# All w1 operands of the first MLP pass formed during the attention, drawn by an estimate of GpSimd's load; query tiles kept without memsets

## The chip, the core and the metric

The kernel runs on one core of a Trainium2 chip. A core has five engines that run side by side: TensorE (PE, with its weight loads as PEld), VectorE (DVE), ScalarE (ACT), GpSimd (POOL) and SyncE (SP). Each takes its instructions in program order and waits on semaphores for the others. In this kernel SP issues every DMA, so SP's order is the order in which transfers start, and a DMA that has to wait for its data holds all later ones.

The metric is the time of one execution in device microseconds (us). Before the change, three runs took 2300.64, 2301.75 and 2305.29 us; the median is 2301.75.

## What is computed

A transformer block with adaptive LayerNorm on x of 2048 x 576 in float32, with 32 query heads of width 18, one shared key and value head, and an MLP of width 4608:

```python
mod = (_silu(c) @ w_mod).reshape(c.shape[0], 6, 1, -1)
sa, ca, ga, sb, cb, gb = (mod[:, 0], mod[:, 1], mod[:, 2], mod[:, 3], mod[:, 4], mod[:, 5])
h = _layernorm(x, axis=-1) * (1 + ca) + sa
x = x + ga * _A_ref(h, A_wq, A_wk, A_wv, A_wo)
h = _layernorm(x, axis=-1) * (1 + cb) + sb
x = x + gb * _B_ref(h, B_w1, B_b1, B_w2, B_b2)
```

`_A_ref` is softmax attention. `_B_ref` applies its own LayerNorm, then `gelu(y @ w1 + b1) @ w2 + b2`.

## The kernel before, in words

**Precision.** Most products are made from parts: a float32 operand is split into a rounded high part and a rest ("hi" and "lo"), and three matmuls (hi x hi, hi x lo, lo x hi) replace one. Forming the parts is a cast and a subtraction. For weights POOL does it, in `two` (lines 692 to 696): `tensor_copy` at L694, `tensor_tensor` at L695.

**Stages.** Stage one (to about 130 us of the trace) does the first LayerNorm and the projections of q, k and v; q goes to the scratch `qscr` in DRAM. Stage two is the attention, to about 1422 us. Stage three is the MLP.

**The attention.** It runs over 32 query tiles n (four heads by 512 tokens each; eight tiles make a token block) and, in each, over 16 chunks kc of 128 keys. For each chunk there are four score matmuls (L824), four exponentials on ACT (L826) and the product with V into `psC` (L813). Beside them PE makes the scores of the next tile once more (L322, L834) so that DVE can take their row maxima (L846, L844), which the softmax needs before that tile starts.

A query tile sits in a buffer `qst`, of which there are three. `load_q(n + 2)` (L858) fills one in chunk 1 of tile n. Rows 0 to 53 of each half of 64 hold parts of q, rows 54 and 55 take the negated maxima, and the rest must be zero. Before the change `new_q` (L127) takes a fresh tile each time and POOL clears rows 32 to 63 of each half (L132). `smax_fin2` (L358), in chunk 13 of the tile before, negates the maxima (ACT L362, DVE L363) and SP writes them into rows 54 and 55 with four DMAs (L367). The scores of the tile wait for these.

**Finishing a tile.** `post_quad` (L613) is a generator that advances one step a chunk during the tile after. Chunk 0: ACT has copied `psC` to `O` (L619), and SP moves the row of sums to `R` (L637). Chunk 3: DVE's reciprocal (L641). Chunk 4: `R` goes to DRAM (`dsum`, L643). Chunk 5: it comes back broadcast as `T` (L647). Chunk 8: POOL multiplies (L651). Chunk 9: POOL makes two parts of the output (`os`, L661 and L662). Chunk 12: four DMAs put them in place for the output projection (`big<-os`, L668).

**Work beside the attention.** `between(n, kc)` (L848) is called once a chunk and sets the program order: the maxima of the next tile, a step of each finishing tile, `load_q`, then a step of `fill` in odd chunks (the late modulation weights, the output projection of a block that is complete, and for the first two blocks the second and third LayerNorm, `ln2_tile`, whose work is on POOL), then a step of `prep`. `prep` holds the generator `weight_parts` (L687): it loads raw weights, forms parts on POOL and sends them to the scratches `w1scr`, `w2scr` and `w2sum`. A store is issued in the step behind the one that formed its parts, and the parts have two buffers (`r2`), so POOL can form a third only when the first has landed in DRAM. Before the change `prep` gets one step in each chunk except 11 and 12, from tile 3 on, whatever else POOL has to do. What is left at chunk 8 of the last tile is emptied at once, and then the operands of the first MLP step are loaded (L867 to 871).

**The MLP.** It is a Strassen-like scheme: seven products of half size instead of eight, with seven operands of w1 (`OPS`, L676) that are blocks, sums and differences of blocks. It runs over two pairs of token blocks, and in each over 18 groups of 256 hidden units, 36 steps v in all; the first pass is v < 18. The operands of one step lie in `W1["r"]`. For groups 0, 1, 2 and 17 (`PRE`, L685) they were formed in the attention and are loaded from `w1scr`. For the other 14 the first pass loads the raw block (`raw_w1`), and POOL and ACT form the operands during the step before (`w1_part`, `w1_sum`, `tail_parts`), and SP stores them for the second pass, which loads all of them.

Of the kernel before, what the change touches and what calls it, by code (L numbers as in the profile page):

```python
# [18 lines left out]
KD = 5  # L19
# [9 lines left out]

@with_exitstack  # L30
def block_kernel(ctx: ExitStack, tc, x, wqkv, wo, w1, b1, w2, b2, c, wmod, ident_in, out):
    nc = tc.nc
    ve, ac, po, pe, sy = nc.vector, nc.scalar, nc.gpsimd, nc.tensor, nc.sync
# [33 lines left out]
    qscr = dr.tile([NB, 2, H * DH, TB], F32, name="qscr")  # L67

# [57 lines left out]

    def new_q(n, e=po):  # L127

        q = QST[n] = pa.tile([128, 2, TB], F32R, name="qst", bufs=3)
        for g in range(2):  # L130
            o = q[64 * g + 32:64 * g + 64]
            e.memset(o.bitcast(F32), 0.0)  # L132

    for n, e in ((0, po), (1, po), (2, ve)):
        new_q(n, e)
# [360 lines left out]
    def late_weights():  # L496
# [3 lines left out]
        yield from mod_bcast(wms[0], BC[:, 2, :], 0.0)  # L500
        gab = px.tile([128, D], F32, name="Z2", padded_shape=[128, 640])
# [111 lines left out]
    def post_quad(n, PV):  # L613
# [49 lines left out]
        if qd < NQ - 1:  # L663
            for _ in range(3):
                yield
            for j in range(4):
                k, r = divmod(4 * qd + j, HC)
                sy.dma_start(A[DH * r:DH * (r + 1), :, k, :].bitcast(F32), os[32 * j:32 * j + DH].bitcast(F32))  # L668
# [9 lines left out]
    def load_w1(i, what, save=False):  # L678
        for w in what.split():
            a = 4 * OPS.index(w) if w in OPS else 28  # L680
            b = min(a + 4, 31)
            ends = W1["r"][:, a:b].bitcast(F32), w1scr[i, :, a:b]
            sy.dma_start(*(ends[::-1] if save else ends))

    PRE = (0, 1, 2, NG - 1)  # L685

    def weight_parts():  # L687
# [10 lines left out]
        def store():  # L698
            sy.dma_start(*late.pop())
# [8 lines left out]
        both = load2(0)  # L708
        yield
        yield  # L710
        for g in range(NG):
            B = [[o[:, 288 * nn:288 * (nn + 1)] for nn in range(2)] for o in both]
            todo = [("mul", 1), ("B", 1, 0), ("mul", 0), ("B", 1, 1)]
            if g < NG - 1:

                b11, b12, b21, b22 = B[1] + B[0]
                todo += [("sub", b11, b12, b11), ("T", 1, b11), None, ("B", 0, 0), ("sub", b12, b22, b12), ("T", 3, b12),
                         ("sub", b11, b22, b11), ("B", 0, 1), None, ("T", 2, b11), ("sub", b11, b21, b11), ("T", 4, b11),
                         None]
            else:  # L720
                todo += [None, ("B", 0, 0), None, ("B", 0, 1), None]
            for it in todo:
                if late:
                    store()
                if it is None:
                    pass
                elif it[0] == "mul":
                    po.tensor_tensor(both[it[1]], both[it[1]], BC[:, 2, :], op=ALU.mult)
                elif it[0] == "sub":
                    po.tensor_tensor(*it[1:], op=ALU.subtract)  # L730
                elif it[0] == "B":
                    _, f, nn = it
                    two(w2scr[g, :, :, f, 288 * nn:288 * (nn + 1)], 1, B[f][nn][:, None, :], [128, 2, 288])
                else:
                    two(w2sum[g, :, it[1] - 1], 1, it[2][:, None, :], [128, 2, 288])
                yield
            if g in PRE:
                raw = px.tile([128, KD - 1, 2, 128], F32, name="r1")
                sy.dma_start(raw.rearrange("p k f c -> p k (f c)"), w1[g][:, :KD - 1])
                tail = px.tile([128, 2, 128], F32, name="r4")  # L740
                sy.dma_start(tail.rearrange("p f c -> p (f c)"), w1[g][:, KD - 1])
                sm = px.tile([128, 2, 128], F32, name="r3")
                yield
                yield

                def blk(f, h):
                    return raw[:, 2 * h:2 * h + 2, f, :]

                for w, how, x, y in (("A11", None, blk(0, 0), None), ("A12", None, blk(0, 1), None),
                                     ("A22", None, blk(1, 1), None), ("S1", ALU.add, blk(1, 0), blk(1, 1)),  # L750
                                     ("S2", ALU.subtract, sm, blk(0, 0)), ("S4", ALU.subtract, blk(0, 1), sm),
                                     ("S3", ALU.subtract, blk(0, 0), blk(1, 0))):
                    if how is not None:
                        po.tensor_tensor(sm, x, y, op=how)
                        x = sm
                    a = 4 * OPS.index(w)
                    two(w1scr[g, :, a:a + 4], 2, x, [128, 4, 128])
                    yield
                    store()
                    yield  # L760
                o = pb.tile([128, 3, 128], F32R, name="r2", bufs=2)
                tail_parts(o, tail, sm[:, 0])
                late.append((w1scr[g, :, 28:31], o.bitcast(F32)))
                yield
                store()
            if g + 1 < NG:
                both = load2(g + 1)
            yield
            yield

    def tail_parts(o, tail, d, e=po):

        e.tensor_tensor(d, tail[:, 0], tail[:, 1], op=ALU.subtract)
        for x, y in ((o[:, :2], tail), (o[:, 2], d)):
            e.tensor_copy(x, y)
            e.tensor_tensor(x[64:], y[64:], x[64:].bitcast(F32), op=ALU.subtract)

# [70 lines left out]
    def between(n, kc):  # L848
# [16 lines left out]
        if n > 2 and kc not in (11, 12):  # L865
            step(prep)
        if kc == 8 and n == NQT - 1:  # L867
# [103 lines left out]
    def wo_end():  # L971
# [8 lines left out]
        W1["pool"] = tc.tile_pool(name="mr", bufs=1, reuse_waits="tile")  # L980
        mr = W1["pool"].__enter__()
        W1["a"] = mr.tile([128, KD, 2, 128], F32, name="w1r")
        W1["s"] = mr.tile([128, 2, 128], F32, name="w1s")
        W1["d"] = mr.tile([128, 128], F32, name="w1d")
        load_w2(0)

    def raw_w1(i):
        sy.dma_start(W1["a"].rearrange("p k f c -> p k (f c)"), w1[i])

    def w1_raw(f, h):  # L990
        return W1["a"][:, 2 * h:2 * h + 2, f, :]

    def w1_part(w, lo):

        if w == "A11":
            o = W1["r"][:, 0:16].rearrange("p (j s) c -> p j s c", s=8)
            src = W1["a"][:, :KD - 1, 0, :].rearrange("p (j s) c -> p j s c", s=2)
            hi, l = o[:, :, 0:2], o[:, :, 2:4]
        else:
            hi, l, src = W1["r"][:, 20:22], W1["r"][:, 22:24], w1_raw(1, 1)  # L1000
        if lo:
            po.tensor_tensor(l, src, hi.bitcast(F32), op=ALU.subtract)
        else:
            ac.activation(hi, src, AF.Copy)

    def w1_sum(w):

        o, a = W1["s"], 4 * OPS.index(w)
        def op(x, y, how=ALU.subtract):
            po.tensor_tensor(o, x, y, op=how)  # L1010
        if w == "S3":
            op(w1_raw(0, 0), w1_raw(1, 0))
        elif w == "S4":
            op(w1_raw(0, 1), W1["r"][:, 4:6].bitcast(F32))
            op(o, W1["r"][:, 6:8].bitcast(F32))
        else:
            op(w1_raw(1, 0), w1_raw(1, 1), ALU.add)
            if w == "S2":
                op(o, w1_raw(0, 0))
        po.tensor_copy(W1["r"][:, a:a + 2], o)  # L1020
        po.tensor_tensor(W1["r"][:, a + 2:a + 4], o, W1["r"][:, a:a + 2].bitcast(F32), op=ALU.subtract)
# [158 lines left out]
    for v in range(NV):  # L1180
# [21 lines left out]
        def w_(w):  # L1202
            if v + 1 < NV and (nxt in PRE or v >= NG):
                load_w1(nxt, w)

        def wt(f, *a):
            if v + 1 < NG and nxt not in PRE:
                f(*a)

        if v == NG:  # L1210
            W1["pool"].__exit__(None, None, None)
# [30 lines left out]
        if 2 < v < NG:  # L1242
            load_w1(v, "S4 tails", True) if v not in PRE else None
# [4 lines left out]
        wt(w1_sum, "S2")  # L1248
# [8 lines left out]
        wt(w1_part, "A11", False)  # L1257
# [6 lines left out]
        wt(w1_sum, "S3")  # L1264
        wt(w1_part, "A11", True)
# [13 lines left out]
        wt(w1_sum, "S1")  # L1279
        wt(load_w1, nxt, "S2", True)  # L1280
# [6 lines left out]
        wt(w1_part, "A22", False)  # L1287
# [5 lines left out]
        wt(w1_part, "A22", True)  # L1293
        wt(load_w1, nxt, "A11 A12 S3", True)
# [7 lines left out]
        wt(w1_sum, "S4")  # L1302
        wt(tail_parts, W1["r"][:, 28:31], W1["a"][:, KD - 1], W1["d"])
# [60 lines left out]
```

## Time and profile before

| | before |
|---|---|
| median of three runs | 2301.75 us |
| the profiled execution | 2300.77 us |
| its span, first to last instruction | 2299.0 us |
| granted TensorE clock, mean | 0.998 |
| busy: PE, DVE, ACT, POOL | 2261.0, 1685.6, 1486.5, 1351.4 us |
| the chain that ended last | PE 92%, ACT 2% |
| bytes moved by DMA | 267.73 MB, mean 116 GB/s |

How to read the profile. A group row gives the line, the engine, the operation, what it writes and reads, the count, the busy time, the mean of one in ns, and then the idle time of the engine just before it with what ended that. Lines are those of the kernel before. A row of the timeline has the start, the duration, the engine, the line and the operation; "x4" is a merged run of four, and "[2.27 <-DMA ...]" is idle time before it with what ended it. "SPq" is SP's queue: the duration is that of issuing, not of the transfer. Matmuls are pipelined and their ends are modelled, so a busy PE is not PE at its peak.

### The profile page before, as it was taken

Reading aid. Unit: us, or ns where it says so; the run is one execution under the profiler, and the core shown is the slowest. Engines: PE = TensorE matmul, PEld = TensorE weight load, DVE = VectorE, ACT = ScalarE, POOL = GpSimd, SP = SyncE. Lnnn points to the kernel's source line nnn. Section 1 sums busy time; section 2 is a strip of 40 time slices with the busy share of each in tenths; the row PEclk is TensorE's granted clock in tenths of the full one; section 3 lists DMA queues with packets and bytes.
Section 4 is the critical chain, followed back from the end, with each engine's and each line's share of the span. In section 5 each row is a group of like instructions: output and inputs, shape, how many; then the busy total and the mean of one; then the engine's idle time right before and its main releaser. Section 6 shows DMA issues by size and latency. Waiting matters only on the chain.

```text
span 2299.0 us, 44576 instructions
## 1 busy us (share of the span) xinstructions
PE 2261.0 (98%) x16310; PEld 1414.3 (62%) x16310; DVE 1685.6 (73%) x3004; ACT 1486.5 (65%) x2851; POOL 1351.4 (59%) x1554
## 2 busy tenths in 40 slices
PE   8999999999999999999999999999999999999999
PEld 5644434454344454344454344899999999989898
DVE  6589999979899979999879992444444456666665
ACT  5569999979999969999979998322222232222221
POOL 6534556345566425657324332588888767777776
PEclk9999999999999999999999999999999999999999
DMA  6221223222222212223123232444444456666663
GB/s 221 87 99 48 76 88 108 89 81 66 75 79 83 92 55 84 83 69 104 60 64 98 73 97 83 162 153 172 149 153 172 147 165 194 181 177 184 178 183 124
DMA packets 160411, 267.73 MB, mean 116 GB/s; under 512 B 26955, under 2 KB 67787, under 8 KB 160193
## 3 DMA queue, kind: packets, MB, share of 16 engines
q1 hardware_dynamic: 160193, 264.89, 36.7%
q8 instruction: 129, 2.11, 0.4%
q14 instruction: 89, 0.73, 0.1%
HBM read 163.45 MB, written 92.24 MB: 111 GB/s over the span
## 4 chain that ended last, share of the span: by engine, by line
PE 92%; ACT 2%; issue 0%; DVE 0%; DMA 0%; SPq 0%; POOL 0%; ACTq 0%
PE psC L813 24%; PE psB L1040 18%; PE psB L824 12%; PE psA L1151 10%; PE psM L322 10%; PE psA L1120 8%; PE psB L834 4%; PE psB L597 2%; ACT P L826 1%; ACT O L619 1%; PE psA L597 1%; PE psB L152 0%; PE psB L251 0%; PE psB L360 0%; DMA qst<-ms 0%
## 5 line engine op out<-in xcount | busy, mean ns | idle before, releaser
L826 ACT ACTIVATE P<-psB 128x512 f32<-128x512 f32 x2048 | 1048.8, 617 | 7.7 <-PE psB L824 6.4
L846 DVE TENSOR_REDUCE mx<-psM 128x1 f32<-128x512 f32 x1476 | 945.6, 683 | 72.1 <-PE psB L824 28.2
L813 PE MATMUL psC<-P,V 128*32 128x256 f32 (+1 forms) x6056 | 599.4, 467 | 13.2 <-ACT O L619 13.2
L824 PE MATMUL psB<-qst,KS 64*128 64x512 f32 x2048 | 598.6, 435 | 5.1 <-DMA qst<-ms 4.7
L322 PE MATMUL psM<-KS,qst 64*128 64x512 f32 x1722 | 592.2, 432 | 0.0
L824 PEld LDWEIGHTS psB<-qst,KS 64*128 64x128 f32 x2048 | 301.3, 185 | 174.4 <-issue 77.6
L1040 PE MATMUL psB<-ops,w1a 128*128 128x512 f32 x1512 | 390.6, 396 | 0.0
L322 PEld LDWEIGHTS psM<-KS,qst 64*128 64x128 f32 x1722 | 283.9, 185 | 115.2 <-DVE mx L844 92.6
L1040 PEld LDWEIGHTS psB<-ops,w1a 128*128 128x128 f32 x1512 | 271.6, 188 | 47.7
L813 PEld LDWEIGHTS psC<-P,V 128*32 128x32 f32 x6056 | 119.7, 108 | 236.9 <-issue 212.1
L1151 PE MATMUL psA<-w2s,big 128*128 128x288 f32 x1488 | 255.4, 295 | 0.0
L1055 ACT ACTIVATE yr<-psB,b1t 128x512 f32<-128x512 f32 x72 | 49.6, 689 | 287.2 <-PE psB L1040 147.1
L1151 PEld LDWEIGHTS psA<-w2s,big 128*128 128x128 f32 x1488 | 221.3, 188 | 6.7
L837 ACT ACTIVATE xc<-psB 128x512 f32<-128x512 f32 x246 | 147.5, 600 | 90.8 <-PE psM L322 61.6
L1155 DVE TENSOR_TENSOR XT<-psA,XT 128x576 f32<-128x576 f32 x152 | 114.2, 752 | 121.5 <-PE psA L1151 121.4
L1055 ACT ACTIVATE gx<-psB,b1t 128x512 f32<-128x512 f32 x72 | 49.6, 689 | 225.8 <-PE psB L1040 76.5
L844 DVE CUSTOM_DVE_ANT_0 xc<-psM,xc 128x512 f32<-128x512 f32 x246 | 167.0, 679 | 4.1 <-PE psM L322 3.4
L1126 DVE TENSOR_TENSOR XT<-psA,XT 128x576 f32<-128x576 f32 x170 | 128.7, 757 | 32.8 <-PE psA L1120 23.5
L834 PEld LDWEIGHTS psB<-KD,qst 64*128 64x128 f32 x246 | 45.1, 183 | 159.2 <-ACT P L826 109.8
L132 POOL MEMSET qst<- 32x1024 f32 x62 | 58.6, 946 | 137.2 <-PE psB L824 91.8
L1059 POOL TENSOR_TENSOR big<-gx,big 128x512 fp32r<-128x512 f32 x72 | 94.8, 1316 | 63.4 <-ACT big L1058 49.6
L834 PE MATMUL psB<-KD,qst 64*128 64x512 f32 x246 | 122.4, 498 | 0.0
(197 smaller groups left out, 2978.1 us busy)
## 6 DMA issues: line engine op xcount, KB each, us to landing
w1a<-w1scr SPq DMA_DIRECT2D x154, 256.0 KB
w1scr<-w1a SPq DMA_DIRECT2D x98, 256.0 KB
w2scr<-r SPq DMA_DIRECT2D x72, 288.0 KB
w2sum<-r SPq DMA_DIRECT2D x68, 288.0 KB
w2s<-w2sum SPq DMA_DIRECT2D x68, 288.0 KB
w2s<-w2scr SPq DMA_DIRECT2D x29, 576.0 KB
qst<-qscr SPq DMA_DIRECT2D x192, 72.0 KB
w2s<-w2scr SPq DMA_DIRECT2D x34, 288.0 KB
```

Source lines behind the costliest of these rows:

```text
L322: pe.matmul(o, QST[n][64 * g:64 * g + 64, p, 128 * qt:128 * (qt + 1)], KS[64 * g:64 * g + 64, 512 * kb:512 * (kb + 1)], start=True, stop=True)
L813: pe.matmul(PVt[n][32 * j:32 * (j + 1), cs], V[:, kc, :], t[:, j, cs], start=(kc == 0 and h0 == 0), stop=(kc == 15), skip_group_check=True)
L824: pe.matmul(t, KS[64 * g:64 * g + 64, 128 * kc:128 * (kc + 1)], QST[n][64 * g:64 * g + 64, i, :], start=True, stop=True)
L826: ac.activation(P[n, kc][:, 2 * i + g, :], t, AF.Exp, scale=SCALE)
L834: pe.matmul(t, QST[n][64 * g:64 * g + 64, p, 128 * qt:128 * (qt + 1)], KD1[64 * g:64 * g + 64, :], start=True, stop=True)
L837: ac.activation(XC[-1], t, AF.Relu)
L844: ve.tensor_tensor_reduce(c, t, c, 1.0, -3.0e38, ALU.add, ALU.max, o)
L846: ve.tensor_reduce(o, t, axis=AX.X, op=ALU.max)
L1040: pe.matmul(o, x, y, start=(first and i == 0), stop=(i == len(terms) - 1), skip_group_check=True)
L1120: pe.matmul(p[:, i, :288], x[:, ts_], W2S[k][:, y], start=(bool(first) and q == 0), stop=(q == 2), skip_group_check=True)
L1126: ve.tensor_tensor(o, p[:, :, :288], o, op=ALU.add)
L1151: pe.matmul(p[:, nn, :288], x, y, start=(q == 0), stop=(q == len(terms) - 1))
```

## The change

It has four parts.

1. POOL is wrapped in `Metered`. Every call through `po` adds an estimate of its duration in ns to a sum: 100 plus the elements per partition times a rate. In each `between` 2,350 is taken off.
2. `prep` is drawn by that sum: a step if it is under 1,500 and the chunk is not 11 or 12, and a second one if it is then under 300. The limit n > 2 goes. `weight_parts` is written anew: four w1 groups first, then w2 and w1 groups in turn, so that all 18 w1 groups are formed in the attention; each step forms one pair of parts (with its sum or scaling, if any), and stores first what the step before formed. The w2 groups wait until `late_weights` has the scale they need (`B2["gate"]`). The last group's `w2sum` is formed as well.
3. The three query tiles are kept: they are cleared once at the start. In later loads, two small DMAs a tile write zeros from the scratch `zscr` over the old maxima in rows 54 and 55.
4. The MLP no longer forms operands of w1: `raw_w1`, `w1_part`, `w1_sum`, `tail_parts` and the stores go, and each step loads the next one's operands from `w1scr`.

Beside these, `post_quad` waits one more step before the four DMAs of the attention output (L668) for n > 2, so that they are issued in chunk 13, behind the maxima of the next tile.

```diff
+class Metered:
+    RATE = {"tensor_copy": 1.0, "memset": 0.9, "tensor_scalar": 3.0}
+    def __getattr__(self, name):
+        f = getattr(self.e, name)
+        def call(out, *a, **k):
+            n = 1
+            for d in out.shape[1:]:
+                n *= d
+            self.load += 100 + n * self.RATE.get(name, 2.35)
+            return f(out, *a, **k)
+        return call
+    def elapse(self, t):
+        self.load = max(0.0, self.load - t)
...
+    zscr = dr.tile([2, 2 * TB], F32, name="zscr")
...
-    def new_q(n, e=po):
-        q = QST[n] = pa.tile([128, 2, TB], F32R, name="qst", bufs=3)
+    for n, e in ((0, po), (1, po), (2, ve)):
+        q = pa.tile([128, 2, TB], F32R, name="qst%d" % n)
         for g in range(2):
-            o = q[64 * g + 32:64 * g + 64]
-            e.memset(o.bitcast(F32), 0.0)
+            e.memset(q[64 * g + 32:64 * g + 64].bitcast(F32), 0.0)
+        QST.update((m, q) for m in range(n, NQT, 3))
+    sy.dma_start(zscr, QST[2][32:34].rearrange("r p t -> r (p t)").bitcast(F32))
...
-        if n not in QST:
-            new_q(n)
         q = QST[n]
         for g in range(2):
             for r in range(3):
...
+            if n > 2:
+                sy.dma_start(q[64 * g + R3:64 * g + R3 + 2].rearrange("r p t -> r (p t)").bitcast(F32), zscr)
...
         if qd < NQ - 1:
-            for _ in range(3):
+            for _ in range(4 if n > 2 else 3):
                 yield
...
         def store():
-            sy.dma_start(*late.pop())
+            while late:
+                sy.dma_start(*late.pop())
...
+        def part2(g):
+            both = load2(g)
+            for _ in range(2):
+                store()
+                yield
...
+            todo = [[("mul", 1), ("B", 1, 0)], [("mul", 0), ("B", 1, 1)],
+                    [("sub", b11, b12, b11), ("T", 1, b11)], [("B", 0, 0)], [("sub", b12, b22, b12), ("T", 3, b12)],
+                    [("sub", b11, b22, b11), ("B", 0, 1)], [("T", 2, b11)], [("sub", b11, b21, b11), ("T", 4, b11)]]
+            for its in todo:
+                store()
...
+                yield
+        def part1(g):
...
+            for w, how, x, y in (("A11", None, blk(0, 0), None), ("A12", None, blk(0, 1), None),
...
+                store()
+                if how is not None:
+                    po.tensor_tensor(sm, x, y, op=how)
+                    x = sm
+                a = 4 * OPS.index(w)
+                two(w1scr[g, :, a:a + 4], 2, x, [128, 4, 128])
+                yield
...
+        for g in range(EARLY):
+            yield from part1(g)
+        while "gate" not in B2:
+            store()
+            yield
         for g in range(NG):
+            yield from part2(g)
+            if g + EARLY < NG:
+                yield from part1(g + EARLY)
+        store()
+
+    EARLY = 4
...
-        if n > 2 and kc not in (11, 12):
+        po.elapse(2350)
+        if kc not in (11, 12) and po.load < 1500:
             step(prep)
+            if po.load < 300 and kc not in (10, 13):
+                step(prep)
...
         def w_(w):
-            if v + 1 < NV and (nxt in PRE or v >= NG):
+            if v + 1 < NV:
                 load_w1(nxt, w)
...
-        wt(w1_sum, "S2")
...
-        wt(load_w1, nxt, "S1 A22", True)
-        if v + 2 < NG and v + 2 not in PRE:
-            raw_w1(v + 2)
```

More of the change, by code (lines that the diff above doesn't have):

```diff
@@ L676, in block_kernel, with load_w1 @@
     OPS = ("A11", "S2", "A12", "S3", "S1", "A22", "S4")
-    def load_w1(i, what, save=False):
+    def load_w1(i, what):
         for w in what.split():
@@ L681, in load_w1 @@
             b = min(a + 4, 31)
-            ends = W1["r"][:, a:b].bitcast(F32), w1scr[i, :, a:b]
-            sy.dma_start(*(ends[::-1] if save else ends))
-    PRE = (0, 1, 2, NG - 1)
+            sy.dma_start(W1["r"][:, a:b].bitcast(F32), w1scr[i, :, a:b])
     def weight_parts():
@@ L706, in load2 @@
             return a, b
-        both = load2(0)
-        yield
-        yield
-        for g in range(NG):
[L712 to L776, printed above, removed]
+        def part2(g):
[3 more added lines that the diff above has]
+                yield
+            B = [[o[:, 288 * nn:288 * (nn + 1)] for nn in range(2)] for o in both]
+            b11, b12, b21, b22 = B[1] + B[0]
+            todo = [[("mul", 1), ("B", 1, 0)], [("mul", 0), ("B", 1, 1)],
[3 more added lines that the diff above has]
+                store()
+                for it in its:
+                    if it[0] == "mul":
+                        po.tensor_tensor(both[it[1]], both[it[1]], BC[:, 2, :], op=ALU.mult)
+                    elif it[0] == "sub":
+                        po.tensor_tensor(*it[1:], op=ALU.subtract)
+                    elif it[0] == "B":
+                        _, f, nn = it
+                        two(w2scr[g, :, :, f, 288 * nn:288 * (nn + 1)], 1, B[f][nn][:, None, :], [128, 2, 288])
+                    else:
+                        two(w2sum[g, :, it[1] - 1], 1, it[2][:, None, :], [128, 2, 288])
+                yield
@@ new lines, in part1, with blk @@
+        def part1(g):
+            raw = px.tile([128, KD - 1, 2, 128], F32, name="r1")
+            sy.dma_start(raw.rearrange("p k f c -> p k (f c)"), w1[g][:, :KD - 1])
+            tail = px.tile([128, 2, 128], F32, name="r4")
+            sy.dma_start(tail.rearrange("p f c -> p (f c)"), w1[g][:, KD - 1])
+            sm = px.tile([128, 2, 128], F32, name="r3")
+            for _ in range(2):
+                store()
+                yield
+            def blk(f, h):
+                return raw[:, 2 * h:2 * h + 2, f, :]
+            for w, how, x, y in (("A11", None, blk(0, 0), None), ("A12", None, blk(0, 1), None),
+                                 ("A22", None, blk(1, 1), None), ("S1", ALU.add, blk(1, 0), blk(1, 1)),
+                                 ("S2", ALU.subtract, sm, blk(0, 0)), ("S4", ALU.subtract, blk(0, 1), sm),
+                                 ("S3", ALU.subtract, blk(0, 0), blk(1, 0))):
+                store()
[6 more added lines that the diff above has]
+            store()
+            o = pb.tile([128, 3, 128], F32R, name="r2", bufs=2)
+            d = sm[:, 0]
+            po.tensor_tensor(d, tail[:, 0], tail[:, 1], op=ALU.subtract)
+            for x, y in ((o[:, :2], tail), (o[:, 2], d)):
+                po.tensor_copy(x, y)
+                po.tensor_tensor(x[64:], y[64:], x[64:].bitcast(F32), op=ALU.subtract)
+            late.append((w1scr[g, :, 28:31], o.bitcast(F32)))
+            yield
```

62 lines of the change are left out of this document (8 added, 54 removed).

## The prediction

> **What bounds the kernel now.** I read the page first, then the windows view (tile by tile and for the MLP), then the waits, then the timeline of SP around the longest PE wait.
>
> ```profile
> PE 2261.0 (98%) x16310; PEld 1414.3 (62%) x16310; DVE 1685.6 (73%) x3004; ACT 1486.5 (65%) x2851; POOL 1351.4 (59%) x1554
> ...
> L826 ACT ACTIVATE P<-psB 128x512 f32<-128x512 f32 x2048 | 1048.8, 617 | 7.7 <-PE psB L824 6.4
> ...
> L132 POOL MEMSET qst<- 32x1024 f32 x62 | 58.6, 946 | 137.2 <-PE psB L824 91.8
> ```
>
> The whole-span shares mix two stages, so the windows view comes next. Its columns are the stretch, its length, then the busy time and count of PE, PEld, DVE, ACT, POOL, then the granted clock, the DMA share and GB/s. The first two rows are the two passes of the MLP; each other row runs from one copy of O (ACT, L619) to the next, which is one query tile of the attention.
>
> ```profile
> 1474.40:1893.10 418.70, 418.70 (x2524) 379.15 (x2523) 203.84 (x307) 118.27 (x197) 339.73 (x428) 1.00 0.46 157
> 1893.10:2281.90 388.80, 388.67 (x2278) 349.70 (x2277) 239.41 (x323) 88.63 (x138) 282.47 (x256) 1.00 0.63 176
> ...
> 294.92:333.05 38.13, 37.67 (x323) 15.29 (x321) 35.45 (x69) 37.36 (x76) 25.72 (x30) 1.00 0.29 89
> 1277.81:1315.94 38.13, 37.67 (x323) 15.29 (x321) 35.45 (x69) 37.36 (x76) 13.54 (x17) 1.00 0.29 90
> 580.78:622.58 41.80, 39.08 (x324) 15.88 (x324) 36.58 (x73) 37.77 (x77) 21.51 (x27) 0.98 0.24 75
> 622.58:662.65 40.07, 40.07 (x332) 16.64 (x332) 36.94 (x75) 37.69 (x76) 22.91 (x27) 0.98 0.30 86
> 662.65:701.56 38.91, 38.45 (x328) 16.08 (x326) 36.37 (x73) 37.60 (x77) 26.96 (x33) 1.00 0.27 81
> 701.56:740.44 38.88, 38.43 (x323) 15.77 (x321) 36.87 (x75) 37.22 (x76) 20.08 (x24) 1.00 0.29 89
> 911.31:952.77 41.46, 38.98 (x328) 16.06 (x326) 36.79 (x74) 37.72 (x77) 26.57 (x32) 1.00 0.22 69
> 952.77:992.04 39.27, 38.81 (x328) 15.93 (x326) 36.80 (x75) 37.60 (x76) 23.00 (x26) 1.00 0.28 88
> 992.04:1030.96 38.92, 38.46 (x328) 16.05 (x326) 36.37 (x73) 37.59 (x77) 26.18 (x33) 1.00 0.26 81
> ```
>
> In the MLP, PE is busy for all of 418.70 us and for 388.67 of 388.80 us. Whatever POOL, ACT or SP stop doing there gives nothing. In the attention a plain tile takes 38.13 us, and ACT works 37.36 of it: ACT is the bound, DVE (35.45) stands close behind, POOL is not near. Two neighbouring pairs are longer than their like: tiles 11 and 12 take 41.80 + 40.07 against 2 x 38.91 of tile 13 (4.05 more), tiles 19 and 20 take 41.46 + 39.27 against 2 x 38.92 of tile 21 (2.89 more). The waits say why:
>
> ```profile
> PE psB L824 <- DMA qst<-ms: 4.7, 3, 2.3
> PEld psB L834 <- ACT P L826: 109.8, 135, 1.4
> DVE R L641 <- DMA R<-O: 10.9, 1, 10.9
> ```
>
> Three times PE waited for the negated maxima (L367) that must land in the next query tile before its scores. SP around the longest, and around the second:
>
> ```profile
> 604.49 2.30 POOL L538 TENSOR_SCALAR Z<-XT,mv,rs 128x576 f32<-128x576 f32 x1
> ...
> 610.24 0.81 POOL L695 TENSOR_TENSOR r<-r,r 128x288 fp32r<-128x288 f32 x1
> ...
> 612.09 0.28 DVE L363 SCALAR_TENSOR_TENSOR ms<-psB,ms 16x128 fp32r<-16x128 f32 x1
> ...
> 611.07 0.52 SPq L699 DMA_DIRECT2D w2scr<-r  x1
> 611.65 3.44 SPq L668 DMA_DIRECT2D big<-os  x4
> 615.19 2.80 SPq L367 DMA_DIRECT2D qst<-ms  x4
> ...
> 619.27 0.62 PE L824 MATMUL psB<-qst,KS 64*128 64x512 f32 x2 [2.27 <-DMA qst<-ms]
> ...
> 941.62 0.34 SPq L699 DMA_DIRECT2D w2sum<-r  x1
> 942.00 3.45 SPq L668 DMA_DIRECT2D big<-os  x4
> 945.56 2.80 SPq L367 DMA_DIRECT2D qst<-ms  x4
> ...
> 949.59 0.59 PE L824 MATMUL psB<-qst,KS 64*128 64x512 f32 x2 [2.02 <-DMA qst<-ms]
> ...
> 325.29 2.82 SPq L367 DMA_DIRECT2D qst<-ms  x4
> ...
> 333.05 0.62 ACT L619 ACTIVATE O<-psC 128x512 f32<-128x512 f32 x1
> ```
>
> The maxima were ready at 612.37, but SP sent them from 615.19: it had stood until 611.07 at a store of prepared weights, whose parts POOL ended at 611.05 behind a LayerNorm tile (L538 and two more), and then issued the attention output (L668, 3.44 us). PE's waits are 2.27 and 2.02 us, which leaves 0.4 of the 4.7 for the third. Usually the maxima go at once, as in the last two rows: 8.38 us before the copy of O ends (325.29 against 333.05 + 0.62).
>
> **The change, part by part.**
>
> *MLP.* Forming w1 there (POOL, ACT, SP) goes, and eight loads of scratch a pair come. I cost this at nothing: PE covers it wholly in the rows above, and the second pass already takes such loads at 388.67 busy of 388.80. If the cover were gone, a late load would show as PE waiting, which in the MLP comes to 0.13 us now.
>
> *POOL in the attention.*
>
> ```profile
> 343.27 0.40 POOL L694 CAST r<-r 128x256 fp32r<-128x256 f32 x1 [1.28 <-DMA w1scr<-r]
> 343.75 0.74 POOL L695 TENSOR_TENSOR r<-r,r 128x256 fp32r<-128x256 f32 x1
> ```
>
> The 58 memsets inside it go (58 x 0.946 = 54.9 us). Fourteen w1 groups come. Each has eight cast-and-rest pairs and four sums; with 0.40 + 0.74 us a pair and 0.74 a sum that is 12 us, 168 us in all. The net of 113 us is hidden if POOL's load alone counts: the two 38.13 us rows have POOL busy 25.72 and 13.54 us, and PE, DVE and ACT the same to the hundredth.
>
> Here a rule of the Trainium skill speaks against the change. "SBUF — State Buffer", section "SBUF: two separate sides", says that VectorE, in a two-port mode or with two SBUF inputs, and GpSimd lock each other out of a shared pair of ports for a whole instruction. By that rule the net POOL time could appear on DVE; the two rows disagree for this mix of DVE work, and it stays a small rival below.
>
> *When work is drawn.* I counted the estimate out of the diff. Stage one leaves a load of about 63,000; all calls together are about 807,000, and 512 chunks take away 512 x 2,350 = 1,203,000. So the first draw falls in tile 2, chunk 13, the last in tile 29, chunk 8. The final emptying loop at tile 31 finds nothing, and the MLP's start keeps its operands. In a chunk with a LayerNorm tile's three calls over 576 (1,828 + 2 x 1,454 = 4,735), the next draws are skipped, and their stores with them.
>
> *The attention output's DMAs.* From tile 4 on they are issued a chunk later, in chunk 13 behind the maxima instead of ahead of them. At 611 and 942 both causes go: no store is drawn there and 3.44 us of issue stand behind. The maxima then leave when ready, 2.8 us earlier at 615.19, which covers the 2.3 us; 3.45 us of issue at 942.00 covers 2.02. The gain is 4.05 + 2.89, and for the third wait of 0.4 us, at the same ratio of 1.6 us lost per us waited (6.94 / 4.3), 0.7: **7.6 us**. Next in line is ACT itself.
>
> *What this pushes.* Behind the 3.45 us now stand, in SP's order, the store of chunk 10's parts, the store of 13's, that of 14's, and then the rows of sums (R, L637) that DVE's reciprocal (L641) takes in chunk 3. There are two `r2` buffers, so chunk 14's parts wait until chunk 10's store has landed.
>
> ```profile
> 333.69 2.48 SPq L637 DMA_DIRECT2D R<-O  x4
> 339.75 0.24 DVE L641 RECIPROCAL R<-R 128x16 f32<-128x16 f32 x1
> ...
> 1390.64 2.48 SPq L637 DMA_DIRECT2D R<-O  x4
> 1394.96 0.25 DVE L641 RECIPROCAL R<-R 128x16 f32<-128x16 f32 x1 [10.88 <-DMA R<-O]
> ...
> 943.75 0.42 POOL L694 CAST r<-w2b 128x288 fp32r<-128x288 f32 x1 [0.16 <-DMA w2sum<-r]
> ...
> 339.51 0.35 SPq L699 DMA_DIRECT2D w1scr<-r  x1
> ...
> 307.35 0.43 SPq L741 DMA_DIRECT2D r<-in_w  x1
> 311.09 0.40 POOL L694 CAST r<-r 128x256 fp32r<-128x256 f32 x1 [5.48 <-DMA r<-in_w]
> ```
>
> With the end of O's copy as zero: the maxima leave at -8.4 and are issued by -5.6, the output by -2.1, chunk 10's store by -1.6. It lands 1.8 us on (941.96 to 943.75), at +0.2. Chunk 14's parts take 1.2 to 2.0 us, their store waits for them until about +2 and is issued by +2.5. Only then come R's 2.48 us of issue and 1.84 us of landing (1393.12 to 1394.96): +6.8, where DVE reaches the reciprocal at +6.08 (339.75). DVE, and behind it the reductions that free psM for PE, would stand 0.7 us. Now R starts at +0.02 and lands 1.8 us early. A weight load drawn in chunk 13 is worse: issued by -1.2 and landing 3.3 us on (307.78 to 311.09), it lets chunk 14 end near +4.8, and R lands 3 us late or more.
>
> I carried SP's and POOL's clocks through tiles 3 to 29 in this way, draw by draw. For the kernel before, the same walk puts the maxima late in tiles 11 and 19 alone, by 1.9 and 1.7 us where the trace has 2.3 and 2.0. For the changed one it gives R late in eight tiles, 10.7 us in sum (3.2 once, 2.0 twice, about 0.9 five times), the maxima late once by 0.4, and LayerNorm inputs late three times, 1.6 us in sum.
>
> Not each us of DVE's delay is lost: PE waits for a bank of ACT 135 times, so ACT has work queued. Below stands zero (all absorbed), above 12.3 us (nothing is). Between them I take 0.4, near tile 14, where 1.42 us more of DVE's work (36.87 against 35.45) made 0.75 us more. That is 12.3 x 0.4 = 4.9, and 0.4 x 1.6 = 0.6 for the maxima: **5.5 us** to pay.
>
> *The rest.* Two zero loads a tile and the store of zeros at the start: 58 issues at about 0.34 us (as 941.62 above) behind `load_q`, whose tile is needed most of a tile later; nothing. Without the memset SP waits at `load_q` for PE's last reads itself, as POOL did before it (91.8 us in its row); nothing.
>
> **The sum.** The profiled execution took 2300.77 us, 1.8 over its span of 2299.0. 2300.77 - 7.6 + 5.5 = 2298.7. It lies 0.98 under the median of the runs, 2301.75; by that, 2299.6.
>
> **Rivals.**
> - *All of the new lateness is absorbed.* For it: ACT's queue, and 0.9 us is under two exponentials of 0.51 (1048.8 / 2048). Against: tile 14's 0.75. Then 2301.75 - 7.6 = 2294.2.
> - *SP falls behind; slower than before.* With up to two groups' parts stored a tile and a half, the stores' landing sets the pace. The store that was issued by 339.86 landed only at 343.27, 3.4 us on, with the query loads in flight, against 1.8. With all landings 1.3 times as long, the walk gives 19.7 us of late R, 6.5 of late maxima, 4.6 of late LayerNorm inputs: 24.3 x 0.4 + 6.5 x 1.6 = 20.1, less 7.6: +12.5, 2314.2. It decides from about 1.15 times on; at twice, the maxima alone are 62 us late and the time passes 2390. "DMA: Bandwidth & Descriptors" of the Trainium skill, "Latency and other measured facts", says that access to HBM goes from 0.2 us to 2 us at high load; the pair 1.8 and 3.4 us agrees in direction.
> - *It doesn't do what it says*: the maxima stay late for another reason, with R on time: no change, 2301.8.
> - *The shared ports.* If all 113 us appeared on DVE and 0.4 of them in the time, +45: about 2347.
>
> **How the numbers follow.** About 0.2%, 4.6 us, is what a measurement of this kernel can tell from no change: faster lies under 2297.1, slower over 2306.4. The forecast has 0.45, of which 0.13 falls under 2297.1, 0.30 within and 0.02 above. Absorbed 0.23, faster. SP behind 0.23, slower, save 0.01. Not doing it 0.06, within. Ports 0.03, slower. Faster 0.36, same 0.37, slower 0.27. The range goes from 2291 (absorbed, with 3 us of spread) to 2320, which takes in the slower rival at 1.3 but not its far end nor the ports; that leaves out about 0.15.
>
> **What would show it.** In the trace after: L824 has no wait for the maxima at tiles 11 and 19, and these tiles take 39 us; DVE at the reciprocal waits for R a few times, by 1 to 3 us; SP issues R later than O; POOL's draws end near tile 29; both MLP passes keep 418.7 and 388.8. I am wrong if the MLP's lengths move, if plain tiles leave 38.13 with R and the maxima on time, or if the maxima are late in many tiles.

## The result, and the profile after

| | before | after |
|---|---|---|
| median of six runs | 2301.56 us | 2317.91 us |
| lowest to highest | 2298.39 to 2305.29 | 2315.85 to 2320.38 |
| the profiled execution, its span | 2300.77, 2299.0 us | 2319.95, 2318.2 us |
| granted TensorE clock, mean | 0.998 | 0.995 |

The ratio is 1.0071, with a 95% interval from 1.0059 to 1.0084: the change makes the kernel about 16 us slower. The forecast was 2299.6. In what follows, line numbers are those of the kernel that a fence is from; in the kernel after, every call on POOL goes through `Metered` and shows as L46.

From the page of the kernel after, the busy time and the groups that answer to those shown of before:

```profile
span 2318.2 us, 44808 instructions
...
PE 2271.3 (98%) x16310; PEld 1416.9 (61%) x16310; DVE 1681.1 (73%) x3004; ACT 1479.5 (64%) x2823; POOL 1301.9 (56%) x1536
...
L846 ACT ACTIVATE P<-psB 128x512 f32<-128x512 f32 x2048 | 1049.5, 614 | 16.9 <-PE psB L844 14.7
...
L343 PE MATMUL psM<-KS,qst 64*128 64x512 f32 x1722 | 596.5, 434 | 9.3 <-DVE mx L866 9.3
...
L46 POOL CAST r<-r 128x256 fp32r<-128x256 f32 (+2 forms) x198 | 77.8, 393 | 228.3 <-DMA w1scr<-r 105.6
```

DVE, ACT and POOL each do less work than before, and the exponentials take as long as ever (614 against 617 ns). PE alone is busy for longer, by 10 us, with the same 16310 matmuls: part of them ran at a lower clock. The new idle times stand in the last column: ACT's exponentials wait for scores (16.9 us, 7.7 before), PE's maxima matmuls wait for DVE (9.3), and POOL's casts wait 105.6 us for stores of w1 parts to land.

The windows view of the kernel after puts the loss in its places. The first five rows are tiles 5, 6, 7, 10 and 13, from one copy of O to the next (columns as before); the last lies in the MLP:

```profile
333.00:374.90 41.90, 39.34 (x327) 15.75 (x325) 36.51 (x71) 37.57 (x75) 23.03 (x37) 1.00 0.45 148
374.90:419.00 44.10, 40.19 (x325) 15.82 (x321) 35.53 (x69) 37.50 (x75) 33.25 (x37) 0.92 0.35 113
419.00:458.30 39.30, 38.84 (x329) 15.95 (x325) 36.58 (x71) 37.38 (x76) 25.07 (x37) 1.00 0.35 116
551.60:595.70 44.10, 40.60 (x325) 16.03 (x321) 36.98 (x74) 37.63 (x76) 32.66 (x43) 0.92 0.32 106
676.10:719.30 43.20, 40.20 (x328) 16.49 (x326) 36.51 (x73) 37.85 (x77) 34.35 (x44) 0.96 0.36 115
...
1476.00:1912.00 436.00, 436.00 (x2637) 395.35 (x2636) 205.48 (x317) 114.09 (x176) 159.96 (x137) 1.00 0.41 135
```

In the MLP, PE is busy for every one of the 436 us, as before, and from the last copy of O to the end of the span it is 876.57 us against 876.70: nothing was won or lost there. Tile 7 is as long as before (39.23 against 39.15 us between the unrounded copies). Set against before in the same way, tile 5 is longer by 2.78 us, tile 6 by 5.96, tile 10 by 5.65, tile 13 by 4.25, tiles 28 and 29 by 1.31 and 1.35; tiles 11, 12, 18 and 19 are shorter, by 1.14, 0.28, 0.80 and 1.74.

What the engines waited for there, in the waits view of the kernel after (columns: total us, times, longest):

```profile
POOL r L46 <- DMA w1scr<-r: 105.6, 32, 16.3
...
POOL r L46 <- DMA r<-in_w: 86.6, 15, 14.5
...
POOL w2b L46 <- DMA w2b<-in_w: 62.8, 16, 8.5
...
DVE R L663 <- DMA R<-O: 20.9, 8, 10.6
...
DVE bst L161 <- POOL Z L46: 7.8, 10, 3.5
...
PE psB L173 <- POOL Z L46: 2.5, 1, 2.5
...
PE psB L844 <- DMA qst<-ms: 1.9, 2, 1.7
```

POOL's own waits cost nothing by themselves. The last four rows do. R is late seven times by 10.3 us in sum (20.9 less the 10.6 at the last tile, which before had too), a LayerNorm tile is late for DVE by up to 3.5 us (L161) and once for PE by 2.5 us (L173), and the maxima are late by 1.7 us once.

How POOL's waits become theirs is read from the timeline. In it, the kernel after in tiles 5 and 6, then in tile 10:

```profile
352.54 0.64 SPq L116 DMA_DIRECT2D bigw<-in_wmod  x1
353.28 14.27 SPq L719 DMA_DIRECT2D w1scr<-r  x5
367.64 2.85 SPq L388 DMA_DIRECT2D qst<-ms  x4
370.60 3.31 SPq L690 DMA_DIRECT2D big<-os  x4
374.01 0.41 SPq L725 DMA_DIRECT2D r<-in_w  x1
374.47 0.42 SPq L725 DMA_DIRECT2D w2b<-in_w  x1
...
380.74 0.64 SPq L719 DMA_DIRECT2D w2scr<-r  x1
381.47 2.52 SPq L659 DMA_DIRECT2D R<-O  x4
...
360.70 0.40 POOL L46 CAST r<-r 128x256 fp32r<-128x256 f32 x1 [6.06 <-DMA w1scr<-r]
...
377.92 1.42 POOL L46 TENSOR_TENSOR w2b<-w2b,BC 128x576 f32<-128x576 f32 x1 [4.52 <-DMA w2b<-in_w]
...
385.90 0.25 DVE L663 RECIPROCAL R<-R 128x16 f32<-128x16 f32 x1 [4.16 <-DMA R<-O]
...
567.99 1.43 POOL L46 TENSOR_TENSOR w2b<-w2b,BC 128x576 f32<-128x576 f32 x1 [5.87 <-DMA w2b<-in_w]
...
576.08 0.46 DVE L161 BATCH_NORM_STATS2 bst<-Z 128x6 f32<-128x288 f32 x1 [3.55 <-POOL Z L46]
```

*Tile 5, maxima.* A load of late modulation weights (L116, 1440 KB) is issued just ahead of the stores of w1 parts. The stores queue behind it: in the trace the load lands at 359.91 and the store behind it, issued by 355.03, at 360.57, 5.5 us on; the store that the prediction reads took 1.8. Both `r2` buffers stay taken, and POOL stands for 6.06 us until 360.70. The parts after that are late, SP stands at their store until 367.6, and the maxima leave only then.

*Tile 6, R.* The raw w2 weights of the next group were issued at 374.47, behind the maxima and the attention output, and POOL took them up at 377.92, after 4.52 us of standing. Their first parts are ready at about 380.7; until then SP stands at their store, with R behind it. R leaves at 381.47, lands at 385.90, and DVE has waited 4.16 us at the reciprocal, with the reductions that free `psM` queued behind.

*Tile 10, LayerNorm.* A load of the same kind, drawn with one step between it and its use, holds POOL for 5.87 us, and behind it in POOL's order stand three calls of a LayerNorm tile. DVE waits 3.55 us for their result. In tile 13 POOL stands for 4.01 us at such a load, until 694.84, and PE waits 2.54 us for a LayerNorm tile, until 708.89.

So the estimate counts POOL's work and not its waits: where POOL stands at a landing, `load` falls on, and more is drawn.

### The profile page after: what moved, and what is told of

It is laid out like the page before. It is cut to its first block, busy times and chain, and to the rows that moved or that the text cites. A ratio compares the mean times of both kernels' runs of the same rounds, so it can differ in the third digit from the quotient of the medians.

```text
span 2318.2 us, 44808 instructions
## 1 busy us (share of the span) xinstructions
PE 2271.3 (98%) x16310; PEld 1416.9 (61%) x16310; DVE 1681.1 (73%) x3004; ACT 1479.5 (64%) x2823; POOL 1301.9 (56%) x1536
## 4 chain that ended last, share of the span: by engine, by line
PE 88%; ACT 3%; POOL 2%; DMA 1%; issue 1%; SPq 1%; DVE 1%; ACTq 0%; POOLq 0%; DVEq 0%
PE psC L833 22%; PE psB L1022 18%; PE psB L844 11%; PE psA L1133 10%; PE psM L343 9%; PE psA L1102 8%; PE psB L854 4%; PE psB L619 2%; ACT P L846 2%; POOL r L46 1%; ACT O L641 1%; PE psA L619 1%; PE psB L173 0%; POOL Z L46 0%; DMA R<-O 0%
## 5 line engine op out<-in xcount | busy, mean ns | idle before, releaser
L846 ACT ACTIVATE P<-psB 128x512 f32<-128x512 f32 x2048 | 1049.5, 614 | 16.9 <-PE psB L844 14.7
L866 DVE TENSOR_REDUCE mx<-psM 128x1 f32<-128x512 f32 x1476 | 945.6, 683 | 78.2 <-PE psM L343 35.5
L46 POOL TENSOR_TENSOR big<-gx,big 128x512 fp32r<-128x512 f32 x72 | 94.6, 1314 | 228.1 <-ACT big L1040 210.3
L46 POOL CAST r<-r 128x256 fp32r<-128x256 f32 (+2 forms) x198 | 77.8, 393 | 228.3 <-DMA w1scr<-r 105.6
L46 POOL TENSOR_TENSOR r<-r,r 128x256 fp32r<-128x256 f32 (+4 forms) x234 | 169.3, 723 | 18.1
L1108 DVE TENSOR_TENSOR XT<-psA,XT 128x576 f32<-128x576 f32 x170 | 128.8, 758 | 32.7 <-PE psA L1102 23.4
```

Source lines behind the costliest of these rows:

```text
L46: return f(out, *a, **k)
L846: ac.activation(P[n, kc][:, 2 * i + g, :], t, AF.Exp, scale=SCALE)
L866: ve.tensor_reduce(o, t, axis=AX.X, op=ALU.max)
```

## The experiments

The leading theory was this chain: parts and raw loads are drawn so close to their landing that POOL and SP stand, and what is queued behind them comes late. Against it stood that POOL's added work itself slows DVE or delays the attention's own POOL steps; that the attention output, moved behind the maxima, does the harm; and that the kept tiles with their zero loads do. All times are medians, beside the runs of the kernel before on the same chip (2301.6 in experiments 1 and 2 and the first two kernels of 6, 2302.62 in 3 to 5 and the third kernel of 6, 2301.87 in 7).

### 1. After, with the attention output issued early again

```diff
-            for _ in range(4 if n > 2 else 3):
+            for _ in range(3):
```

> The changed kernel with one thing undone: the four DMAs of the attention output go again in chunk 12, ahead of the maxima of the next tile (three steps of waiting for every tile). Theory A (parts that wait for stores to land, and raw loads, make POOL and SP late; the order on SP only decides which of R and the maxima pays): R is on time nearly everywhere, but the maxima come late in about ten tiles, some 20 us in sum by the walk over the queues, and the time is the same as that of the changed kernel or worse, 2318 to 2340 us. Rival B (the later output DMAs are what makes R late, and the draws are harmless): the waits for R go and the time falls to about 2305 us or less.

Measured: 2333.38 us, ratio 1.0141 (1.0127 to 1.0156), 15.5 us slower than the kernel after. From its waits view:

```profile
PE psB L844 <- DMA qst<-ms: 24.5, 8, 6.1
...
DVE R L663 <- DMA R<-O: 11.0, 1, 11.0
```

R is now late only at the last tile, but the maxima are late eight times, by 24.5 us. Moving the output is no part of the damage; it chooses which transfer is late, and it chooses the cheaper one. The rival that blames it falls.

### 2. After, with a third buffer for parts

```diff
-    sel = pa.tile([128, 128], F32, name="sel")
+    sel = pa.tile([128, 1], F32, name="sel")
...
-            T = px.tile([128, TB], F32, name="T")
+            hold = px.tile([128, 2, TB], F32R, name="os")
+            T = hold[:, 1].bitcast(F32)
...
-            o = pb.tile(shape, F32R, name="r2", bufs=2)
+            o = pb.tile(shape, F32R, name="r2", bufs=3)
```

`T` moves into the half of `os` that is written last, which makes room.

> The changed kernel with a third buffer for the parts (r2), so that POOL waits for the store before the last but one; room for it comes from laying the broadcast sums T into the second half of the output tile and from a selector of one column. The same draws in the same chunks. Theory A: waits for stores were the pace; R is late in tile 6 alone (about 3.7 us, a raw load), LayerNorm inputs hardly, and the time is 2296 to 2304 us. Rival B (POOL has too much work in the attention): the draws and their durations are unchanged, so the time stays at 2314 to 2320 us. Rival C (raw loads drawn one or two chunks before their use are the pace): tiles 6, 10 and 13 keep most of their excess, 2308 to 2314 us.

Measured: 2303.41 us, ratio 1.0010 (1.0001 to 1.0019), 14.5 us faster than the kernel after. What is left lies in tiles 6 (5.82 us longer than before), 10 (3.34), 29 and 5 (0.55 and 0.34). In tile 6 the timeline shows why:

```profile
381.42 0.25 DVE L664 RECIPROCAL R<-R 128x16 f32<-128x16 f32 x1 [3.66 <-DMA R<-O]
```

R is late there by the raw load, which a third buffer for parts doesn't bring earlier.

### 3. The room alone

Experiment 2 with `bufs=2`.

> Control for e2_third_buffer: the changed kernel with the room made (T laid into the output tile, the selector of one column) and still two buffers for the parts. Theory A: the buffer was what helped, so this is the changed kernel's time, 2314 to 2320 us, with the excess of tiles 5, 6, 10 and 13. Rival: the room-making itself helped, 2303 us.

Measured: 2318.36 us, ratio 1.0067 (1.0052 to 1.0083), the time of the kernel after. The gain of experiment 2 belongs to the third buffer, not to the new place of `T`. The loss is spread over the tiles in another way (tile 5 now 4.45 us, tile 6 2.16), so which tile pays depends on small shifts; how much is paid in all doesn't.

### 4. After, without the second draw in a chunk

```diff
-            if po.load < 300 and kc not in (10, 13):
-                step(prep)
```

> The changed kernel without the second draw of a chunk, so that a raw load has two whole chunks before its use; two buffers as in the change, and the draws now end in chunk 7 of tile 31. Theory A with raw loads as the second wait: tile 10 and tile 13 lose their excess, R is late in tiles 6, 8, 24 and 26 to 29 by 0.7 to 1.9 us each, and the time is 2295 to 2305 us. Rival (stores alone, or POOL's work alone): 2310 us or more.

Measured: 2306.76 us, ratio 1.0022 (1.0013 to 1.0030), 11.2 us faster than the kernel after. With a step a chunk at most, a store has one chunk, some 2.4 us (38.13 / 16), before its buffer is asked for, and a raw load has two before its data is. The edit also spreads POOL's work, and this run doesn't tell the two apart. Tile 10 loses all of its excess, tile 13 keeps 1.81 us, and tile 27, where R is late by 2.67 us, is 3.68 us longer than before: two buffers remain. That leaves the time 1.8 us above the range that was expected.

### 5. Both: third buffer and no second draw

> The changed kernel with the third buffer and without the second draw. All operands of w1 are still formed in the attention, so POOL's work is that of the change. Theory A: no wait is left in the attention, the late output DMAs keep their gain, and the time is that of e3_before_output_late, 2291 to 2297 us. Rival (POOL's 113 us more of work cost time in themselves): above 2300 us.

Measured: 2293.89 us, ratio 0.9964 (0.9951 to 0.9976). The windows view of a plain tile near the end of the attention, and the waits for LayerNorm tiles and for stores of w1 parts:

```profile
1270.00:1308.10 38.10, 37.64 (x327) 15.30 (x323) 35.49 (x69) 37.38 (x75) 21.26 (x31) 1.00 0.34 106
```

```profile
DVE bst L161 <- POOL Z L46: 3.1, 8, 0.6
...
POOL r L46 <- DMA w1scr<-r: 88.4, 19, 10.2
```

The same w1 and w2 parts are formed on POOL in the attention (1302.1 us busy in all), and no tile is longer than before by more than 0.72 us. The plain tile has 21.26 us of POOL where before has 13.54, and DVE, ACT and its length are the same to 0.04 us. So POOL's load by itself costs nothing, and no lockout of DVE shows in this mix of work. Nor does POOL's standing by itself: it still stands 88.4 us at the stores of w1 parts, against 105.6. What is gone is the lateness behind it: R is late at the last tile alone, no LayerNorm tile by more than 0.6 us, and PE has no wait for the maxima. What cost 24 us was standing at landings while something urgent was queued behind.

### 6. Before, with only the output late; with only the tiles kept; with both

```diff
-            for _ in range(3):
+            for _ in range(4 if n > 2 else 3):
```

> The kernel before with one part of the change alone: the output DMAs one chunk later, behind the maxima, for tiles after the third. Theory A: the maxima are on time in tiles 11 and 19, R too, and the time falls by the 7.6 us of the prediction, to about 2294 us. Rival (the gain of the prediction is not there, or R becomes late by the 3.45 us of issue that now stand before it): 2301 us or more.

> The kernel before with another part alone: the three query tiles kept, without memsets in the attention, zeros for the old maxima by two small DMAs a tile. Theory A: no engine waited for the memsets where it counted, so nothing changes: 2299 to 2304 us, with the waits for the maxima in tiles 11 and 19 still there. Rival (the memsets held POOL back, or the zero loads hold SP): 2296 us or less, or 2306 us or more.

> The kernel before with the two parts that gained or cost nothing: the output DMAs behind the maxima, and the query tiles kept. Theory A: 2291 to 2296 us, as e3_before_output_late, with no wait for the maxima. Rival (the zero loads cost once the maxima are first): 2297 us or more.

Measured: the late output 2293.62 us, ratio 0.9966 (0.9954 to 0.9979); the kept tiles without memsets 2301.40, ratio 1.0002 (0.9993 to 1.0011); both 2293.74, ratio 0.9964 (0.9951 to 0.9976). With the late output tile 11 is 2.72 us shorter, 12 0.79, 18 0.82 and 19 2.42, and the rest stand still. The memsets and the zero loads make no difference. The kernel after is therefore 8 us of gain and 24.3 us of loss (2317.91 - 2293.62), all of the loss from the drawing of `prep`. The one line of the late output, alone, is as fast as anything run here, and it beats both kernels.

### 7. What a late DVE costs: the same DVE work, in lumps and spread

On the kernel with the late output and the kept tiles, reductions of V into a tile that nobody reads are added, 54 in each kernel. They delay DVE by a known amount, with no change to any other engine.

```diff
+        if 3 < n < 31 and kc == 3:
+            for _ in range(2):
+                ve.tensor_reduce(dum, V.rearrange("p a b -> p (a b)"), axis=AX.X, op=ALU.max)
```

The second has one in chunk 3 and one in chunk 9 (`kc in (3, 9)`); the third has six in chunk 3 of every third tile (`n % 3 == 1`).

> What a late R costs, measured by itself: e8_before_late_and_kept (2293.7 us) with two reductions over V more on VectorE (128x512 from SBUF to a column that nobody reads) in chunk 3 of tiles 4 to 30, in the place of the reciprocal that waited for R. An estimate from the reduction over psM is 0.64 us each, 1.3 us a tile, 34 us in 27 tiles. The prediction's share of 0.4 (ScalarE has work queued): +14 us, 2307. Theory that a lump on VectorE is not absorbed: +24 us or more, 2318 or more.

> The same two reductions a tile, one in chunk 3 and one in chunk 9, so that the work is that of e9_dve_lump in two halves. If only the sum counts, the same time as e9_dve_lump. If the length of one stop counts (work queued at ScalarE covers a short one), clearly less: about half of e9's addition.

> Six such reductions in chunk 3 of every third tile from 4 to 28 (nine tiles, some 3.8 us each, 35 us in all): as long as the wait for R in tile 6 of the changed kernel. If the TensorE clock that is granted after a stop of that length makes the loss longer than the stop, as in that tile (+5.96 us for 4.16), the addition is about 1.4 times the work, some 45 to 55 us, and the windows after the stops show a clock near 0.5. If not, at most 35 us, with the clock at 1.0.

The group rows (by line) of the three:

```profile
L858 DVE TENSOR_REDUCE dum<-V 128x1 f32<-128x512 f32 x54 | 35.5, 657 | 0.9
```

```profile
L858 DVE TENSOR_REDUCE dum<-V 128x1 f32<-128x512 f32 x54 | 35.2, 652 | 0.0
```

```profile
L858 DVE TENSOR_REDUCE dum<-V 128x1 f32<-128x512 f32 x54 | 36.5, 676 | 1.6
```

| the same 54 reductions | DVE work | median | more than without | per us of work | in a plain tile |
|---|---|---|---|---|---|
| two in one place | 35.5 us | 2317.12 | 23.4 us | 0.66 | 1.00 us for 1.31 |
| one in each of two places | 35.2 us | 2305.09 | 11.4 us | 0.32 | 0.45 us for 1.30 |
| six in one place, every third tile | 36.5 us | 2341.69 | 48.0 us | 1.3 | 6.05 us for 4.06 |

The ratios to before are 1.0064 (1.0050 to 1.0078), 1.0015 (1.0006 to 1.0024) and 1.0175 (1.0161 to 1.0189). What a us of DVE's delay costs is no constant: it grows by four times with the length of the lump. The second kernel falls to about half of the first's addition, as the theory of one long stop had it; the first is 0.9 us short of the 2318 that the theory of no absorption set as its least. In both the granted clock is 1.00 all through the attention, so the step from 0.32 to 0.66 doesn't come from the clock. The third kernel repeats what tile 6 of the kernel after does, and the windows around one of its lumps show the second half of the price:

```profile
296.00:300.20 4.20, 4.20 (x38) 1.65 (x30) 3.97 (x9) 4.12 (x9) 2.08 (x3) 1.00 0.61 192
300.20:303.60 3.40, 0.01 (x2) 0.00 (x0) 3.29 (x6) 1.13 (x3) 2.26 (x2) 0.86 0.46 166
303.60:309.00 5.40, 5.38 (x26) 1.72 (x28) 3.65 (x7) 2.17 (x4) 0.93 (x2) 0.50 0.53 168
309.00:317.00 8.00, 8.00 (x70) 3.52 (x72) 6.88 (x13) 7.30 (x15) 7.69 (x9) 0.97 0.10 35
```

PE stops for 3.40 us, and in the 5.40 us after that it runs at a granted clock of 0.50: 26 matmuls, where at full clock 4.20 us took 38. The tile is 6.1 us longer for a stop of 3.4. Of the nine lumps, the one in tile 25, where PE has matmuls of the output projection beside, stops PE for only 1.49 us, from 1195.61 to 1197.10; the clock stays at 1.00, and the tile is 2.29 us longer. The other eight tiles, with the clock at 0.50 behind each stop, are 5.14 to 6.36 us longer.

## Why the prediction was wrong, by its own steps

**Right.** *The MLP*: nothing, as costed. *The memsets and zero loads*: nothing; experiment 6 has 1.0002. *The output's gain*: 7.6 us forecast, 8.0 measured alone, but not quite from where it was summed. Of the four tiles that were named, 11, 12 and 19 are shorter and tile 20 is not (39.28 and 39.26 us); tile 18, 0.82 us shorter, was not named. The third wait of 0.4 us, priced at 0.7, lies at 134.45 us, at the start of the first tile, and is still there after (0.20). That the sum fits so well is in part luck. *POOL's load and the shared ports*: no cost; experiment 5. (That holds for this mix: most of DVE's work there, the reductions of `psM`, has one input, and a mix with two inputs in SBUF is not shown.) *When work is drawn*: the first raw load is issued at 251.14 us, and the last store ends its issue at 1361.08, in tiles 2 and 29, as counted. *Late R*: the walk through SP's and POOL's clocks gave 10.7 us in sum over eight tiles, the trace has 10.3 in seven, with the longest 4.16 against a forecast "3.2 once". The place of the damage was right: what stands ahead of R on SP.

**Wrong: the term "to pay", 5.5 us forecast.** In the two profiled executions, the tiles of the kernel after are 25.88 us longer in sum than those with the late output alone. By what was late in them:

| late | forecast | lateness measured | paid |
|---|---|---|---|
| R (tiles 6, 8, 11 and 12, 16, 28, 29) | 10.7 x 0.4 = 4.3 | 9.79 us | 11.7 us |
| LayerNorm inputs (10, 13, 19 and 20) | 1.6 x 0.4 = 0.6 | 3.55 + 2.54 + 1.18 = 7.27 us | 11.0 us |
| the maxima, and R by 0.48 (tile 5) | 0.4 x 1.6 = 0.6 | 1.67 + 0.48 us | 2.75 us |
| none found (27) | | | 0.4 us |

Two steps of it failed, and the first counts for most.

*"Between them I take 0.4, near tile 14".* The bounds were written as zero, all absorbed, and 12.3 us, nothing absorbed, so that a us late could cost one us at most. The runs show 0.66 to 0.77 for 1.3 us in a lump and 1.3 to 1.5 for 4 us. Tile 14's 1.42 us of additional DVE work were the wrong row: that work is spread (pieces of 0.21 to 0.45 us between 703.14 and 733.16), and experiment 7 gives 0.32 for spread work, close to the 0.4 taken, and twice that and more for the same work in one piece. The prediction's own first part held the sign of it: a wait of PE for the maxima was priced at 1.6, above one, and a long wait of DVE stops PE in the same way. At 0.4, with every lateness as measured, the sum would be 17.06 x 0.4 + 0.48 x 0.4 + 1.67 x 1.6 = 9.7 us: still about 16 us short of 25.88. The price also leaves out the clock, for which the prediction has no term: 15.87 of the 25.88 us lie in tiles 6, 10 and 13, the three behind whose stops of PE (3.46, 3.10 and 2.54 us) the granted clock fell to 0.50. The stops are 9.10 us of this, and 6.8 us come on top.

*"LayerNorm inputs late three times, 1.6 us in sum".* The three places were right, tiles 10, 13 and 19, and the size was wrong by 4.5 times. The walk had raw loads landing in 3.3 us of their issue; at tile 10 the load issued by 564.17 ended POOL's wait at 567.99, 3.8 us on, and three calls of the draw, to 570.78, still stood ahead of the LayerNorm tile. Also missed was the 1440 KB load of modulation weights (L116), which was in the trace of before (L91, 345.11) and which the prediction doesn't name as a transfer that stores queue behind. By the timeline it makes the 1.67 us of tile 5; no run tests it alone.

**The rivals.** "SP falls behind; slower than before", priced 2314.2, is what happened. Its cause was put at all landings being 1.3 times as long; the runs show a few long ones (a store behind a large load, a raw load drawn with one step between it and its use) and a higher price for each. Its sum had 24.3 us late at 0.4; what is there is 17.5 us late, of which the 17.06 of R and LayerNorm cost 22.7 (1.3 for each).

## What to carry to other kernels

A draw that follows an estimate of an engine's work has to count its waits as well, or keep a distance between a transfer's issue and the step that takes its data: a third buffer and one draw a chunk took away the whole 24 us here, with the same work on the same engine. What is added to an in-order queue is priced by what stands behind it when it waits. And a late input isn't priced by the share of idle time: ask how long it stops the bounding engine at one place, for short delays are partly absorbed, and one that makes PE stand for long enough costs the clock as well.

## What the runs showed of the hardware

The granted clock falls after a short stop of PE, and stays low for longer than the stop. In the kernel after, around the stop in tile 6 (from 383.29 to 386.75 us), and behind that of tile 13 (2.54 us, to 708.89):

```profile
380.00:383.20 3.20, 3.20 (x28) 1.17 (x24) 1.73 (x3) 3.13 (x7) 3.12 (x4) 1.00 0.28 95
383.20:387.00 3.80, 0.34 (x4) 0.26 (x2) 1.10 (x3) 1.19 (x3) 3.66 (x5) 0.77 0.37 119
387.00:392.00 5.00, 5.00 (x26) 1.34 (x26) 3.38 (x7) 2.17 (x4) 4.31 (x7) 0.50 0.54 182
392.00:400.00 8.00, 8.00 (x72) 3.56 (x72) 6.97 (x14) 7.41 (x15) 7.61 (x10) 1.00 0.35 121
...
709.00:714.00 5.00, 5.00 (x32) 2.29 (x34) 2.59 (x5) 3.28 (x7) 4.77 (x8) 0.66 0.26 56
```

And in the kernel before, behind its two waits for the maxima, of 2.27 and 2.02 us:

```profile
619.30:624.30 5.00, 5.00 (x33) 2.00 (x37) 2.47 (x5) 4.26 (x9) 0.00 (x0) 0.66 0.09 34
949.60:954.60 5.00, 4.54 (x39) 1.72 (x41) 3.44 (x7) 4.37 (x9) 0.00 (x0) 1.00 0.18 62
```

A stop of 3.46 us is followed by 5 us at half clock, where PE counts as busy for all of it and ends 26 matmuls, where the 8 us after them, at full clock, take 72, or 45 in 5 us. Stops of 2.54 and 2.27 us are followed by a mean of 0.66, which is about 3.4 us at half clock; a stop of 2.02 by none. The loss of tile 6, 5.96 us, is the stop and some 2.5 us of slow clock.

The length of the stop alone doesn't decide it. Where the clock is low in the attention, it is so for 3.41 or 6.83 us at a time, and in one trace the beginnings of these times lie whole multiples of 3.41 us apart (385.23 and 576.38 in the kernel after: 56 times 3.413). Cut at these places, the rows show what stood before a fall. The first is the kernel after, in tile 6; the next two are the kernel before, in tile 19; the last two are the kernel with only the tiles kept (experiment 6), in the same tile:

```profile
381.82:385.23 3.41, 1.47 (x14) 0.49 (x11) 0.00 (x0) 2.57 (x5) 3.19 (x6) 1.00 0.28 91
...
945.03:948.44 3.41, 2.54 (x17) 0.85 (x17) 3.26 (x7) 2.85 (x6) 2.73 (x4) 1.00 0.23 49
948.44:951.85 3.41, 2.26 (x23) 0.95 (x23) 1.47 (x4) 1.62 (x4) 0.00 (x0) 1.00 0.25 88
...
943.95:947.37 3.42, 1.74 (x13) 0.46 (x11) 3.08 (x6) 2.06 (x4) 0.13 (x1) 1.00 0.12 28
947.37:954.19 6.82, 6.45 (x33) 2.43 (x37) 2.72 (x6) 4.49 (x9) 0.00 (x0) 0.50 0.13 43
```

In tile 6 the clock falls at 385.23, in the middle of the stop, after a stretch of 3.41 us in which PE stood for 1.94. In tile 19 the stop is of the same length in both kernels (2.02 and 2.05 us). In one it is shared out over two stretches, 0.87 and 1.15 us, and the clock holds; in the other 1.67 us of it fall into one stretch, the clock falls for 6.83 us, and tiles 19 and 20 are 1.33 and 0.99 us longer. All thirteen traces together, from 140 to 2280 us, have 8108 such stretches at full clock. The clock fell after all 28 in which PE stood for 1.58 us or more, and after none in which it stood for 1.49 us or less. So in this kernel a stop is at risk from about 1.6 us on, and whether the clock falls depends on where the stop lies.

The Trainium skill, page "TensorE: Matmul & The Clock Gate", Part 1, says that the clock goes to half after at least one idle window of about 3.4 us, and that the window runs freely. The length of the stretches and their free running agree; the idleness doesn't, as a stretch in which PE stood for 1.58 of its 3.41 us was enough, so here the measurement decides.
